# Linear attention's sums over the keys, head by head in four column tiles of the matmul array

## The chip, the cores and the metric

The kernel runs on one core of a Trainium2 chip. The metric is the device time of one execution in microseconds, the median of several runs. The core has a matmul engine (TensorE, PE in the profile, with its weight loads shown apart as PEld), three engines for elementwise work (VectorE or DVE, ScalarE or ACT, GpSimd or POOL) and a queue engine (SP) that issues most transfers. TensorE reads its operands from SBUF and writes to PSUM, which has eight banks of 128 partitions by 512 float32 values.

## The reference

Two layers with the same weights, each an attention step and a dense step. All is float32; S = 2048 rows, D = 576, H = 32 heads of Dh = 18, F = 4608.

```python
    def _A_ref(x, wqkv, w_phi, wo):
        ...
        pq = jnp.einsum("bhsd,hdf->bhsf", q, w_phi)
        pk = jnp.einsum("bhsd,hdf->bhsf", k, w_phi)
        phi_q = jnp.concatenate([_softmax(pq, axis=-1), _softmax(-pq, axis=-1)], axis=-1)
        phi_k = jnp.concatenate([_softmax(pk, axis=-1), _softmax(-pk, axis=-1)], axis=-1)
        kv = jnp.einsum("bhsf,bhsd->bhfd", phi_k, v)
        z  = jnp.einsum("bhsf->bhf", phi_k)
        num = jnp.einsum("bhqf,bhfd->bhqd", phi_q, kv)
        den = jnp.einsum("bhqf,bhf->bhq", phi_q, z)[..., None] + 1e-6
        o = num / den
        return (lambda x, *d: x.transpose(*d))(o, 0, 2, 1, 3).reshape(B, S, D) @ wo
    ...
    x = x + _A_ref(_layernorm(x, axis=-1), A_wqkv, A_w_phi, A_wo)
    x = x + _B_ref(_layernorm(x, axis=-1), B_w1, B_b1, B_w2, B_b2)
    x = x + _A_ref(_layernorm(x, axis=-1), A_wqkv, A_w_phi, A_wo)
    x = x + _B_ref(_layernorm(x, axis=-1), B_w1, B_b1, B_w2, B_b2)
```

`_B_ref` is `relu(x @ w1 + b1) ** 2 @ w2 + b2`. What the change touches is `kv` and `z`: for each head the sum over all 2048 keys of the outer products of 36 features (18 of each softmax) with 18 values and a one.

## The kernel before

The rows are worked in NB = 4 blocks of TB = 512, each of NT = 4 tiles of 128. Large products take their operands split into a high and a low part (float32r, one pass each). The products of the key sums stay in plain float32; the profile shows each of them as two loads of weights and two matmul records.

*Where the sums are made.* `make_v` multiplies a tile's rows with the weights of v and copies the result out of PSUM to a buffer `v`, in five groups of heads (four of 7 heads, 126 columns, and one of 4 heads, 72), each group with a column of ones ahead. `soft` and `soft_k` make the tile's features `e`, two softmaxes of 576 columns. `kv_tile` then multiplies, group by group, the ones and values (weights, up to 127 columns) with both softmaxes' features of that group (moved, 2 x 126 columns). This gives all pairs of heads in the group; only the blocks on the diagonal are wanted. The five products lie in three PSUM banks.

*Where they are kept.* All of layer 0's 16 tiles, and the last two blocks' 8 tiles of layer 1, add up in PSUM banks `kvp` (taken from the banks `acc0` to `acc2` that the dense layers use otherwise), which a product of zeros opens. The first two blocks of layer 1 are summed while the dense layers use these banks; each tile goes through three work tiles and is added to `kv` in SBUF by VectorE. `wtile` hands out work tiles in PSUM: two banks of the tag `w` at all times, and in turn with them those that `spare` names when the dense layers rest.

*What is made of them.* `sums_operands` stands between the last keys of a layer and its queries. It broadcasts the sums of the ones to all partitions (`sel` as weights, results `z`, copied to `zb`), turns the rest (`kt`), masks the blocks on the diagonal (`ko`) and splits them (`kbh`, `kbl`). `g_phi` divides the query features by their denominators with `zb`: VectorE and POOL each multiply, then TensorE turns the result (`g_out`).

*The order.* Generators are woven by hand (`weave`, `lagged`), and a scheduler orders the instructions of every engine by the order in which they are written where it has a choice. `barrier` writes the last keys of a layer and the first queries: names that begin with `t0` and `t1` are the barriers of the two layers. Names `m_0` to `m_3` are the dense layers of a block, `a_` a block's attention in their background, `K_` and `k_` keys, `kv_0k` to `kv_3k` the background's work tiles for the sums, `fo` the folding of w_phi into the weights at the start.

Of the kernel before, what the change touches and what calls it, by code (L numbers as in the profile page):

```python
# [21 lines left out]
def layers_kernel(  # L22
# [34 lines left out]
    HP = D // 2                      # 288  # L57
# [13 lines left out]
    # Work tiles in PSUM: two banks at all times; the banks of the dense layers too while these rest.  # L71
# [47 lines left out]
    sel = cst.tile([GW + 1, P], F32, name="sel")  # L119
    nc.vector.memset(sel, 0.0)  # L120
    nc.vector.memset(sel[0:1, :], 1.0)
    zero = cst.tile([1, P], F32R, name="zero")
    nc.vector.tensor_copy(zero, sel[32:33, :])
    zeros = zero.unsqueeze(1).to_broadcast([1, TB // P, P])
# [9 lines left out]
    def rows_twice(src, c0, n):  # L134
        """The last DT rows of src, columns c0.., on both halves of the partitions."""
# [8 lines left out]
    def g_fold(kpair):  # L144
        """Makes wf, and of it the pieces for k at once."""
# [89 lines left out]
    def g_norm(x_of, dst, name, then=None):  # L235
        """x_of(t): tile t of the rows. A step to a tile, and one for the features beyond KC * P."""
# [32 lines left out]
        def turn_rest(h):  # L269
            """The features beyond KC * P of half h of the rows."""  # L270
# [41 lines left out]
    def make_v(x, t, pair, name):  # L312
        vt = sb.tile([P, NG, GW + 1], F32, tag="v", name=f"{name}v{t}", bufs=4)
        nc.gpsimd.memset(vt[:, :, 0:1], 1.0)
        for half in range(2):
            pt = project(x, t, pair[half], f"{name}pv{half}{t}")
            a = half * HP
            while a < (half + 1) * HP:
                g, o = divmod(a, GW)
                e = min((half + 1) * HP, (g + 1) * GW)  # L320
                q = a - half * HP
                if o == 0 and a + 2 * GW <= (half + 1) * HP:
                    nc.scalar.activation(vt[:, g : g + 2, 1:],
                                         pt[:, q : q + 2 * GW].rearrange("p (g d) -> p g d", d=GW), AF.Copy)
                    a += 2 * GW
                else:
                    nc.scalar.activation(vt[:, g, 1 + o : 1 + o + e - a], pt[:, q : q + e - a], AF.Copy)
                    a = e
# [44 lines left out]
    sums = {}  # L373
    pairs = [range(g, min(g + 2, NG)) for g in range(0, NG, 2)]

    def pair_view(pt):
        return pt[: GW + 1, : 4 * GW].rearrange("p (g s f) -> p g s f", g=2, s=2)

    def kv_tile(layer, vt, e, name):
        """Adds a tile's keys: in PSUM where the dense layers rest (in the second layer for the last  # L380
        two blocks only), else in SBUF."""
        if layer not in sums:
            sums[layer] = {"kv": cst.tile([GW + 1, NG, 2, GW], F32, name=f"kv{layer}", tag="kv"), "n": 0}
# [4 lines left out]
        if n == first:  # L388
            st["ps"] = [ps_a.tile([P, TB], F32, tag=f"acc{i}", name=f"kvp{layer}{i}")
                        for i in range(len(pairs))]  # L390
            for pt, gs in zip(st["ps"], pairs):
                m = gw[gs[0]] + 1
                nc.tensor.matmul(pt[:m], zero[:, :m], zeros, start=True, stop=False)
# [423 lines left out]
```

## Time and profile before

| | |
|---|---|
| median of 3 runs | 2694.05 us (2693.41 to 2697.58) |
| span of the profiled execution | 2693.9 us |
| TensorE matmuls busy | 2614.6 us, 97% |
| TensorE weight loads busy | 2211.8 us, 82% |
| VectorE busy | 1574.4 us, 58% |
| ScalarE busy | 1065.3 us, 40% |
| GpSimd busy | 605.8 us, 22% |
| mean granted clock of TensorE | 0.989 |

The profiled execution's own time is its span of 2693.9 us; the runs' times have 2693.41 to 2697.58 beside it. The core is the only one. A row of the lines or of the time line names start, duration, engine, line, operation, what is written and read (out<-in) and the shape; a matmul's duration reaches to the modelled end of its result, so matmuls overlap and the distance between starts is what one costs. "idle before" is the idle time of the engine ahead of the group, with what ended it.

### The profile page before, as it was taken

The numbers are of one execution on the slowest core, as the hardware profiler recorded it, in microseconds if no ns is written. First come the engines' busy times: TensorE is split into PE (matmuls) and PEld (weight loads), VectorE is DVE, ScalarE is ACT, GpSimd is POOL, SyncE is SP. The second block draws the span as 40 slices with busy tenths as digits, with TensorE's granted clock in tenths as the row PEclk, the third lists the DMA queues.
The fourth block names the chain that finished last, engine by engine and source line by source line (L and its number), as shares of the span: only waits on it lengthen the run. The fifth ranks groups of instructions, "written<-read, shape, count | busy, mean of one in ns | idle before, by whom it ended". The sixth has DMA issues, their size and how long they took to land. (4 is left out here: it accounts for less than half of the span.)

```text
span 2693.9 us, 36380 instructions
## 1 busy us (share of the span) xinstructions
PE 2614.6 (97%) x13364; PEld 2211.8 (82%) x13364; DVE 1574.4 (58%) x2561; ACT 1065.3 (40%) x1837; POOL 605.8 (22%) x647
## 2 busy tenths in 40 slices
PE   6998999999999999999999989999999999999998
PEld 5997788888878888788888977888888887888887
DVE  5668944365764567547544688444854476444343
ACT  3334343344433444434443333434434343433433
POOL 1443411112311123112211333111321123111110
PEclk8998999999999999999999989999999999999999
DMA  6211233352333532334333113333432343234332
GB/s 208 89 32 45 74 110 101 98 180 84 109 112 97 171 110 82 112 97 132 113 95 109 43 57 114 87 100 102 154 118 86 102 160 97 84 101 128 98 97 74
DMA packets 289021, 280.26 MB, mean 104 GB/s; under 512 B 18697, under 2 KB 230153, under 8 KB 286793
## 3 DMA queue, kind: packets, MB, share of 16 engines
q1 hardware_dynamic: 288841, 277.92, 34.0%
q8 instruction: 105, 1.72, 0.3%
q14 instruction: 75, 0.61, 0.1%
HBM read 246.90 MB, written 30.97 MB: 103 GB/s over the span
## 5 line engine op out<-in xcount | busy, mean ns | idle before, releaser
L605 PE MATMUL m_0ph<-a_0nh,m_0h 128*128 128x512 f32 (+1 forms) x760 | 231.6, 387 | 0.0
L605 PE MATMUL m_2ph<-a_2nh,m_2h 128*128 128x512 f32 (+1 forms) x760 | 228.2, 383 | 0.1
L634 PE MATMUL m_3acc<-m_3s,m_3hb 128*128 128x512 f32 x864 | 214.2, 395 | 3.0 <-DVE m_3hb L616 1.8
L634 PE MATMUL m_0acc<-m_0s,m_0hb 128*128 128x512 f32 x864 | 214.7, 395 | 2.5 <-DVE m_0hb L616 1.1
L634 PE MATMUL m_1acc<-m_1s,m_1hb 128*128 128x512 f32 x864 | 213.3, 394 | 2.6 <-DVE m_1hb L615 1.8
L634 PE MATMUL m_2acc<-m_2s,m_2hb 128*128 128x512 f32 x864 | 213.2, 394 | 0.9 <-DVE m_2hb L615 0.7
L634 PEld LDWEIGHTS m_0acc<-m_0s,m_0hb 128*128 128x128 f32 x864 | 161.0, 188 | 43.4 <-DVE m_0hb L616 4.2
L634 PEld LDWEIGHTS m_3acc<-m_3s,m_3hb 128*128 128x128 f32 x864 | 160.9, 188 | 43.1 <-DVE m_3hb L616 4.2
L634 PEld LDWEIGHTS m_1acc<-m_1s,m_1hb 128*128 128x128 f32 x864 | 161.3, 188 | 42.1 <-DVE m_1hb L615 3.2
L634 PEld LDWEIGHTS m_2acc<-m_2s,m_2hb 128*128 128x128 f32 x864 | 161.3, 188 | 40.3 <-DVE m_2hb L615 2.2
L605 PEld LDWEIGHTS m_0ph<-a_0nh,m_0h 128*128 128x128 f32 x760 | 141.0, 190 | 28.5 <-DVE m_0h L589 0.4
L605 PEld LDWEIGHTS m_2ph<-a_2nh,m_2h 128*128 128x128 f32 x760 | 139.6, 188 | 28.8 <-DVE m_2h L589 1.0
L589 DVE TENSOR_TENSOR m_2h<-m_2r,m_2h 128x640 fp32r<-128x640 f32 x72 | 61.5, 854 | 165.4 <-ACT m_2h L588 165.4
L589 DVE TENSOR_TENSOR m_1h<-m_1r,m_1h 128x640 fp32r<-128x640 f32 x72 | 61.0, 848 | 162.5 <-ACT m_1h L588 162.5
L589 DVE TENSOR_TENSOR m_3h<-m_3r,m_3h 128x640 fp32r<-128x640 f32 x72 | 60.8, 844 | 160.8 <-ACT m_3h L588 160.8
L589 DVE TENSOR_TENSOR m_0h<-m_0r,m_0h 128x640 fp32r<-128x640 f32 x72 | 62.7, 870 | 145.9 <-ACT m_0h L588 139.2
L593 POOL TENSOR_TENSOR m_3s<-m_3r,m_3s 128x64 fp32r<-128x64 f32 x72 | 57.3, 797 | 355.2 <-ACT m_3s L591 349.6
L593 POOL TENSOR_TENSOR m_2s<-m_2r,m_2s 128x64 fp32r<-128x64 f32 x72 | 55.9, 777 | 360.9 <-ACT m_2s L591 355.4
L593 POOL TENSOR_TENSOR m_1s<-m_1r,m_1s 128x64 fp32r<-128x64 f32 x72 | 58.0, 805 | 343.8 <-ACT m_1s L591 341.7
L593 POOL TENSOR_TENSOR m_0s<-m_0r,m_0s 128x64 fp32r<-128x64 f32 x72 | 53.3, 741 | 346.3 <-ACT m_0s L591 323.8
L611 ACT ACTIVATE m_0hr<-m_0ph,b1t 128x512 f32<-128x512 f32 x72 | 49.6, 689 | 193.9 <-PE m_0ph L605 184.7
L611 ACT ACTIVATE m_3hr<-m_3ph,b1t 128x512 f32<-128x512 f32 x72 | 49.7, 690 | 192.4 <-PE m_3ph L605 187.8
(1527 smaller groups left out, 6949.8 us busy)
## 6 DMA issues: line engine op xcount, KB each, us to landing
m_3r<-in_B_w SPq DMA_DIRECT2D x72, 288.0 KB
m_2r<-in_B_w SPq DMA_DIRECT2D x72, 288.0 KB
m_0r<-in_B_w SPq DMA_DIRECT2D x72, 288.0 KB
m_1r<-in_B_w SPq DMA_DIRECT2D x72, 288.0 KB
m_3r<-in_B_w SPq DMA_DIRECT2D x72, 256.0 KB
m_2r<-in_B_w SPq DMA_DIRECT2D x72, 256.0 KB
m_0r<-in_B_w SPq DMA_DIRECT2D x72, 256.0 KB
m_1r<-in_B_w SPq DMA_DIRECT2D x72, 256.0 KB
```

The costliest lines, as they stand in the source:

```text
L589: nc.vector.tensor_sub(l1, r1, h1.bitcast(F32))
L593: nc.gpsimd.tensor_sub(s2[:, D : D + DT], r2[:, R:], s2[:, R:D].bitcast(F32))
L605: nc.tensor.matmul(ph[:, cols], a, m, start=(k == 0), stop=(k == 3 * KC + 1))
L611: nc.scalar.activation(hr, ph, AF.Relu, bias=b1t[:, f : f + 1])
L634: nc.tensor.matmul(acc[t], a[:, rows], m, start=(begin and k == 0), stop=(end and k == 2))
```

## The change

The sums are made head by head. `v` now holds for each head a one and its 18 values, 19 columns (`VW`), and 13 columns of zeros behind the last head. `kv_tile` issues 32 products in place of 5: weights are the 32 columns of `v` from a head's first on (its own 19 and 13 that belong to the next head), moved are the head's own 2 x 18 feature columns, and the result goes to 32 partitions, in the column tile q of four (`tile_position=(0, 32 * q)`). Heads 7q to 7q + 6 go to column tile q at places j = 0 to 6; heads 28 to 31 go to the four column tiles at place j = 7. All of it fills 288 columns of one bank, which a tile of keys in the background copies or adds with one instruction instead of three; in PSUM it takes one bank, and two more become work tiles (`spare`). The product of zeros is one of 288 columns instead of three of 512.

`make_v` copies each half of v with one instruction, where five were needed for both. `sums_operands` works from the new layout: `top` has a one at the first row of each column tile and broadcasts the sums of ones (12 products), 2 transposes turn both softmaxes' sums of 28 heads, and for the last 4 heads a product of VectorE (`kq`) puts each on its own quarter of partitions, and 2 products with `place` bring them to their rows.

```diff
-    sel = cst.tile([GW + 1, P], F32, name="sel")
...
+    top = cst.tile([P, NQ], F32, name="top")
...
+    place = cst.tile([P, NQ, DH], F32, name="place")
...
+    quarter = cst.tile([P, NQ], F32, name="quarter")
...
-    zeros = zero.unsqueeze(1).to_broadcast([1, TB // P, P])
+    zeros = zero[:, : 2 * DH].unsqueeze(1).to_broadcast([1, NS, 2 * DH])
...
     def make_v(x, t, pair, name):
-        vt = sb.tile([P, NG, GW + 1], F32, tag="v", name=f"{name}v{t}", bufs=4)
-        nc.gpsimd.memset(vt[:, :, 0:1], 1.0)
+        vt = sb.tile([P, H * VW + 32 - VW], F32, tag="v", name=f"{name}v{t}", bufs=4)
+        v3 = vt[:, : H * VW].rearrange("p (h d) -> p h d", d=VW)
+        nc.gpsimd.memset(v3[:, :, 0:1], 1.0)
+        nc.gpsimd.memset(vt[:, H * VW :], 0.0)
         for half in range(2):
             pt = project(x, t, pair[half], f"{name}pv{half}{t}")
...
+            nc.scalar.activation(v3[:, half * H // 2 : (half + 1) * H // 2, 1:],
+                                 pt[:, :HP].rearrange("p (h d) -> p h d", d=DH), AF.Copy)
...
+    def head(q, j):
+        return q * HG + j if j < HG else NQ * HG + q
...
+            st["ps"] = ps_a.tile([P, TB], F32, tag="acc0", name=f"kvp{layer}")
+            nc.tensor.matmul(st["ps"][:, : 2 * NS * DH], zero, zeros, start=True, stop=True)
         stay, last = n >= first, n == NB * NT - 1
-        for i, gs in enumerate(pairs):
-            pt = st["ps"][i] if stay else wtile(f"{name}k{i}")
-            po = pair_view(pt)
-            for g in gs:
-                nc.tensor.matmul(po[: gw[g] + 1, g - gs[0], :, : gw[g]], vt[:, g, : gw[g] + 1],
-                                 e[:, :, g * GW : g * GW + gw[g]],
-                                 start=not stay, stop=(not stay or (last and g == gs[-1])))
...
+        pt = st["ps"] if stay else wtile(f"{name}k")
+        po = pt[:, : 2 * NS * DH].rearrange("p (s j f) -> p s j f", s=2, f=DH)
+        for j in range(NS):
+            for q in range(NQ):
+                h = head(q, j)
+                nc.tensor.matmul(po[32 * q : 32 * q + 32, :, j], vt[:, h * VW : h * VW + 32],
+                                 e[:, :, h * DH : (h + 1) * DH], start=not stay, stop=True,
+                                 tile_position=(0, 32 * q), skip_group_check=True)
+        if stay and not last:
+            return
+        if (last and first == 0) or n == 0:
+            nc.scalar.activation(kv, po, AF.Copy)
+        else:
+            nc.vector.tensor_add(kv, po, kv)
...
+        for s in range(2):
+            pt = wtile(f"z{layer}{s}")
+            for q in range(NQ):
+                nc.tensor.matmul(pt[:, q * GW : (q + 1) * GW], top[:, q : q + 1].to_broadcast([P, P]),
+                                 kv[:, s, :HG], start=True, stop=True)
...
+            nc.tensor.transpose(pt[:GW, :P], kv[:, s, :HG].rearrange("p j f -> p (j f)"), ident)
...
-    spare["tags"] = ["acc3", "acc4", "h"]
+    spare["tags"] = ["acc1", "acc2", "acc3", "acc4", "h"]
```

On TensorE, at the first tile of keys of the first layer, before and after (`n_1p` is a transpose of the next block's norm, `v_0pv` the product for the tile's v):

```order
L265 MATMUL n_1p_653<-ident,n_1n_565 128x128 x4
L399 MATMUL kvp_672<-K_0_0e,v_0v_473 127x252 x2
L399 MATMUL kvp_673<-K_0_0e,v_0v_473 127x252 x2
L399 MATMUL kvp_674<-K_0_0e,v_0v_473 73x2x72
L308 MATMUL v_0pv_685<-w0v0h,n_0h 128x288
```

```order
L284 MATMUL n_1p_662<-ident,n_1n_576 128x128 x4
L408 MATMUL kvp_681<-K_0_0e,v_0v_486 32x2x18 x32
L327 MATMUL v_0pv_718<-w0v0h,n_0h 128x288
L327 MATMUL v_0pv_718<-w0v0l,n_0h 128x288
L327 MATMUL v_0pv_718<-w0v0h,n_0l 128x288
```

The place is the same; five products to three banks have become 32 to one.

On TensorE, in the second layer, in the background of a block's dense layers (`m_0acc` and `m_0ph` are their products), before and after:

```order
L627 MATMUL m_0acc_8068<-m_0hb_8738,m_0s_7_8716 128x512 x2
L399 MATMUL kv_2_0k_8857<-k_2K0e,v_2v_8372 127x252 x2
L399 MATMUL kv_2_0k_8861<-k_2K0e,v_2v_8372 127x252 x2
L605 MATMUL m_0ph_8880<-a_0nh,m_0h_9_8873 128x512
L605 MATMUL m_0ph_8880<-a_0nl,m_0h_9_8873 128x512
L399 MATMUL kv_2_0k_8865<-k_2K0e,v_2v_8372 73x2x72
L605 MATMUL m_0ph_8880<-a_0nh,m_0h_9_8873 128x512 x2
```

```order
L649 MATMUL m_0acc_8558<-m_0hb_9220,m_0s_7_9198 128x512 x2
L408 MATMUL kv_2_0k<-k_2K0e,v_2v_8862 32x2x18 x32
L627 MATMUL m_0ph_9385<-a_0nh,m_0h_9_9378 128x512
L627 MATMUL m_0ph_9385<-a_0nl,m_0h_9_9378 128x512
L627 MATMUL m_0ph_9385<-a_0nh,m_0h_9_9378 128x512 x2
```

The tile's third part, which stood two products of the dense layers later, is gone; the tile is one run.

On TensorE, from the last keys of the first layer on (`t0q2qp` are products for the queries of another block), before and after:

```order
L399 MATMUL kvp_674<-k_3K3e,t0v_2245 73x2x72
L425 MATMUL z_2333<-kv_671,sel 128x252 x2
L440 MATMUL kt_2346<-ident,kv_671 126x127
L425 MATMUL z_2338<-kv_671,sel 128x252 x2
L425 MATMUL z_2342<-kv_671,sel 128x2x72
L440 MATMUL kt_2346<-ident,kv_671 126x127 x3
L440 MATMUL kt_2355<-ident,kv_671 126x127 x4
L440 MATMUL kt_2364<-ident,kv_671 72x73 x2
L308 MATMUL t0q2qp_2401<-t0q1h,n_2h 128x288
```

```order
L408 MATMUL kvp_681<-k_3K3e,t0v_2575 32x2x18 x32
L327 MATMUL t0q2qp_2883<-t0q0h,n_2h 128x288
L327 MATMUL t0q2qp_2883<-t0q0l,n_2h 128x288
L327 MATMUL t0q2qp_2883<-t0q0h,n_2l 128x288
L327 MATMUL t0q2qp_2883<-t0q0h,n_2h 128x288
L327 MATMUL t0q2qp_2883<-t0q0l,n_2h 128x288
L428 MATMUL z_2740<-kv_680,top 128x126 x4
L428 MATMUL z_2746<-kv_680,top 128x126 x4
L437 MATMUL z_2752<-kv_680,top 128x2x18 x4
L449 MATMUL kt_2758<-ident,kv_680 126x128
L449 MATMUL kt_2764<-ident,kv_680 126x128
```

Five products for the other block's queries now stand ahead of the broadcasts, which are twelve and no longer stand among the transposes; of these two are left.

More of the change, by code (lines that the diff above doesn't have):

```diff
@@ L57, in layers_kernel @@
     HP = D // 2
+    VW = DH + 1
+    NQ = P // 32
+    NS = H // NQ
+    assert VW <= 32 and NS == HG + 1 and NG == NQ + 1
     cst = ctx.enter_context(tc.tile_pool(name="cst", bufs=1))
@@ L373, in layers_kernel @@
     sums = {}
-    pairs = [range(g, min(g + 2, NG)) for g in range(0, NG, 2)]
-    def pair_view(pt):
-        return pt[: GW + 1, : 4 * GW].rearrange("p (g s f) -> p g s f", g=2, s=2)
+    def head(q, j):
+        return q * HG + j if j < HG else NQ * HG + q
     def kv_tile(layer, vt, e, name):
         if layer not in sums:
-            sums[layer] = {"kv": cst.tile([GW + 1, NG, 2, GW], F32, name=f"kv{layer}", tag="kv"), "n": 0}
+            sums[layer] = {"kv": cst.tile([P, 2, NS, DH], F32, name=f"kv{layer}", tag="kv"), "n": 0}
         st = sums[layer]
@@ L388, in kv_tile @@
         if n == first:
[L389 to L393, printed above, removed]
-        stay, last = n >= first, n == NB * NT - 1
-        for i, gs in enumerate(pairs):
-            pt = st["ps"][i] if stay else wtile(f"{name}k{i}")
-            po = pair_view(pt)
-            for g in gs:
-                nc.tensor.matmul(po[: gw[g] + 1, g - gs[0], :, : gw[g]], vt[:, g, : gw[g] + 1],
-                                 e[:, :, g * GW : g * GW + gw[g]],
-                                 start=not stay, stop=(not stay or (last and g == gs[-1])))
-            w = gw[gs[0]]
-            src = po[: w + 1, : len(gs), :, :w]
-            dst = kv[: w + 1, gs[0] : gs[-1] + 1, :, :w]
-            if stay and not last:
-                continue
-            if (last and first == 0) or n == 0:
-                if i % 2:
-                    nc.vector.tensor_copy(dst, src)
-                else:
-                    nc.scalar.activation(dst, src, AF.Copy)
-            else:
-                nc.vector.tensor_add(dst, src, dst)
+            st["ps"] = ps_a.tile([P, TB], F32, tag="acc0", name=f"kvp{layer}")
+            nc.tensor.matmul(st["ps"][:, : 2 * NS * DH], zero, zeros, start=True, stop=True)
+        stay, last = n >= first, n == NB * NT - 1
+        pt = st["ps"] if stay else wtile(f"{name}k")
[12 more added lines that the diff above has]
+            nc.vector.tensor_add(kv, po, kv)
     def sums_operands(layer):
@@ L433, in sums_operands @@
-        last = NG - 1
-        for i, batch in enumerate([[(0, g) for g in range(last)], [(1, g) for g in range(last)],
-                                   [(0, last), (1, last)]]):
-            w, n = gw[batch[0][1]], len(batch)
-            pt = wtile(f"kt{layer}{i}")
-            p3 = pt[:, : n * (w + 1)].rearrange("p (j m) -> p j m", m=w + 1)
-            for j, (s, g) in enumerate(batch):
-                nc.tensor.transpose(p3[:w, j], kv[: w + 1, g, s, :w], ident[: w + 1, : w + 1])
-            own = sb.tile([P, TB], F32, tag="hr", name=f"ko{layer}{i}", bufs=2)
-            own = own[:w, : n * w].rearrange("p (j m) -> p j m", m=w)
-            nc.vector.tensor_mul(own, p3[:w, :, 1:], mask[:w, :w].unsqueeze(1).to_broadcast([w, n, w]))
-            hi, lo = (k[:w, i, :last, :w] if i < 2 else k[:w, :, last, :w] for k in (kbh, kbl))
+        last = NG - 1
@@ L445, in sums_operands, with keep @@
+        p3 = pt[:, : 2 * NQ * DH].rearrange("p (s q f) -> p s q f", s=2, q=NQ)
+        for q in range(NQ):
+            nc.tensor.matmul(p3[:, :, q], top[:, q : q + 1].to_broadcast([P, P]), kv[:, :, HG],
+                             start=True, stop=True)
+        nc.scalar.activation(zb[:, :, NQ * GW :], p3.rearrange("p s q f -> p s (q f)"), AF.Copy)
+        def keep(own, parts):
+            hi, lo = parts
             nc.scalar.activation(hi, own, AF.Copy)
             nc.vector.tensor_sub(lo, own, hi.bitcast(F32))
+        for s in range(2):
+            pt = wtile(f"kt{layer}{s}")
+            nc.tensor.transpose(pt[:GW, :P], kv[:, s, :HG].rearrange("p j f -> p (j f)"), ident)
+            own = sb.tile([P, TB], F32, tag="hr", name=f"ko{layer}{s}", bufs=2)
+            own = own[:GW, : NQ * GW].rearrange("p (q j d) -> p q j d", q=NQ, j=HG)
+            src = pt[:GW, :P].rearrange("p (q d) -> p q d", q=NQ)[:, :, 1 : 1 + DH]
+            nc.vector.tensor_mul(own, src.unsqueeze(2).to_broadcast([GW, NQ, HG, DH]),
+                                 mask.rearrange("p (j d) -> p j d", j=HG).unsqueeze(1)
+                                 .to_broadcast([GW, NQ, HG, DH]))
+            keep(own.rearrange("p q j d -> p q (j d)"), [k[:, s, :last] for k in (kbh, kbl)])
@@ new lines, in sums_operands @@
+        w = gw[last]
+        own = sb.tile([P, TB], F32, tag="hr", name=f"kq{layer}", bufs=2)
+        own = own[:, : 2 * w].rearrange("p (s q f) -> p s q f", s=2, q=NQ)
+        nc.vector.tensor_mul(own, kv[:, :, HG].unsqueeze(2).to_broadcast([P, 2, NQ, DH]),
+                             quarter.unsqueeze(1).unsqueeze(3).to_broadcast([P, 2, NQ, DH]))
+        pt = wtile(f"kt{layer}2")
+        p3 = pt[:w, : 2 * w].rearrange("p (s n) -> p s n", s=2)
+        for s in range(2):
+            nc.tensor.matmul(p3[:, s], own[:, s].rearrange("p q f -> p (q f)"),
+                             place.rearrange("p q d -> p (q d)"), start=True, stop=True)
@@ L447, in sums_operands @@
+        keep(p3, [k[:w, :, last, :w] for k in (kbh, kbl)])
         sums[layer].update(zb=zb, kb=(kbh, kbl))
```

47 lines of the change are left out of this document (19 added, 28 removed).

## The prediction

> **What bounds the kernel now.** I read the page's busy shares first, then the clock and the slices, then windows along the span, then the lines of the key sums by tile, and last the waits of the two stretches between keys and queries.
>
> ```profile
> PE 2614.6 (97%) x13364; PEld 2211.8 (82%) x13364; DVE 1574.4 (58%) x2561; ACT 1065.3 (40%) x1837; POOL 605.8 (22%) x647
> PE   6998999999999999999999989999999999999998
> PEclk8998999999999999999999989999999999999999
> ```
>
> TensorE (PE) is busy for 97% of the span and its clock is at full grant nearly throughout. Only three places show less than nine tenths: the start, 200 to 300 us, and 1550 to 1650 us. So the time is TensorE's work plus 79 us in which it stands idle. What the change takes from TensorE, or from what TensorE waits for, comes off the end.
>
> The key sums, by windows on their line alone (window, length, PE busy and records, weight loads, clock, DMA):
>
> ```profile
> 0.00:218.00 218.00, 25.51 (x120) 20.68 (x120) 0.95 0.32 104
> 218.00:232.00 14.00, 8.11 (x40) 6.88 (x40) 1.00 0.21 58
> 640.00:700.00 60.00, 9.15 (x40) 6.78 (x40) 1.00 0.43 130
> 960.00:1022.00 62.00, 9.61 (x40) 6.89 (x40) 0.94 0.39 121
> 1470.00:1500.00 30.00, 8.54 (x40) 6.89 (x40) 1.00 0.45 139
> 1538.00:1552.00 14.00, 8.11 (x40) 6.88 (x40) 1.00 0.18 53
> ```
>
> That is 320 records, ten to a tile of 128 keys, so 32 tiles. Five float32 products make ten records, so each product is two loads of weights and two matmul records. The busy time there overlaps its neighbours; what a tile takes from TensorE is the distance between the starts around it:
>
> ```profile
> 79.48 2.11 PE L399 MATMUL kvp<-K_1e,v_0v 128*127 128x252 f32 x10
> 81.43 0.60 PE L265 MATMUL n_1p<-ident,n_1n 128*128 128x128 f32 x4
> ```
>
> One tile costs 81.43 - 79.48 = 1.95 us. It moves 4 x 252 + 144 = 1152 columns twice, so 2304 columns in 1.95 us, 0.85 ns for each column of a record.
>
> **The change, part by part.** *Key sums.* In place of 10 records with 73 to 127 columns of weights come 32 products, so 64 records, each with 32 columns of weights and 36 moved columns. That is 32 x 36 = 1152 columns again, twice: moved one after the other they cost the same 1.95 us, and the change gains only if the four column tiles work side by side, and loses if something other than the moving sets the step. No row shows a matmul in a column tile or one this narrow. The nearest rows are these:
>
> ```profile
> 16.41 1.86 PEld L178 LDWEIGHTS fo<-phi,ft 126*128 126x128 f32 x16 [1.03 <-DVE ft L169]
> 18.19 0.47 PEld L167 LDWEIGHTS fp<-ident,fr 128*126 128x126 f32 x4
> 18.63 0.53 PEld L178 LDWEIGHTS fo<-phi,ft 72*128 72x128 f32 x4
> 18.73 0.56 PE L178 MATMUL fo<-phi,ft 72*128 72x72 f32 x4
> 813.76 0.11 PEld L521 LDWEIGHTS a_0pt<-ident,a_0Q0e 128*72 128x72 f32 x1 [0.29 <-DVE a_0fl L523]
> 813.79 0.12 PEld L521 LDWEIGHTS a_0pt<-ident,a_0Q1e 128*72 128x72 f32 x1
> 268.86 0.27 PE L521 MATMUL t0opt<-ident,t0fQ3e 128*126 128x128 f32 x1
> 268.89 0.48 PE L535 MATMUL t0opn<-t0ofh,kbh 126*126 126x512 f32 x1
> ```
>
> In the folding of w_phi 16 loads of 128 columns take 18.19 - 16.41 = 1.78 us, 0.111 each. Where only 72 columns are moved (18.73) the four records still fill 0.56 us beside loads that fill 0.53: the load sets the step there and the moving is hidden. Loads do get shorter with fewer columns: those of 72 columns at 813.76 start 0.03 apart. So a load of 32 columns is about 0.111 x 32 / 128 = 0.028 us, and moving 36 columns is 36 x 0.85 = 0.030 us. The shortest step from one matmul to the next with other weights is 0.03 (268.86 to 268.89).
>
> Bounds for a tile: all four column tiles side by side, 64 x 0.030 / 4 = 0.49 us; load and moving never together, 64 x 0.058 = 3.7 us. I exclude a step of 0.111 (7.1 us), because the loads of 72 columns show that the load shrinks. Between them I take 64 x 0.027 = 1.73 us: both parts overlap as they do in the folding, and the step is the last pair of rows, which lies at or a little under load and moving alone. That is 0.22 us less for each tile. It counts where TensorE has no slack: in all tiles except the last three of each layer, behind which TensorE waits for others in any case (below). 26 x 0.22 = -6 us, between -38 (26 x 1.46) and +46 (26 x 1.75).
>
> *Waits for PSUM in the background of the dense layers.* There the tile needs three of the two work banks, now one:
>
> ```profile
>   DVE kv L413: 4.7, 3
> 969.73 1.86 PE L399 MATMUL kv_0k<-k_2K0e,v_2v 128*127 128x252 f32 x8
> 975.08 0.76 PE L399 MATMUL kv_0k<-k_2K0e,v_2v 128*73 128x144 f32 x2 [3.02 <-DVE kv L413]
> 965.00:985.00 20.00, 16.98 (x67) 13.75 (x66) 10.47 (x14) 6.00 (x9) 4.78 (x4) 0.83 0.18 53
> 985.00:1005.00 20.00, 20.00 (x111) 17.47 (x110) 15.32 (x18) 9.42 (x14) 5.78 (x6) 1.00 0.39 128
> ```
>
> TensorE stood 4.7 us in three places for the adds of the first two parts, 3.0 of them at 975.08, queued on VectorE. Around that wait the clock fell to 0.83 over 20 us, a half grant for 6.8 us; at most 3.8 of these lie outside the idle time and cost 1.9. Together 6.6. One add is left to each tile, which can still hold a bank when VectorE is late, so I take -6 (0 to -6.6). VectorE's adds shrink from 1152 columns to 288 on the way, which hides behind TensorE.
>
> *Zero fill.* Three products of 512 columns become one of 288:
>
> ```profile
> 1477.42 0.96 PE L393 MATMUL kvp<-zero 1*127 1x512 f32 x3
> 1478.31 2.21 PE L399 MATMUL kvp<-k_0K0e,v_prevv 128*127 128x252 f32 x10
> ```
>
> 0.89 us becomes some 0.15: -0.7. The first layer's lies at 2.4 us, ahead of the first rows, and costs nothing either way. The new constants (memsets and selections on VectorE and POOL) lie there too, under the wait for the first rows of x.
>
> *From the last keys to phi(q), twice.* The chain is copy of the sums, broadcast products, copies to zb, then POOL's first product:
>
> ```profile
> 227.87 2.11 PE L399 MATMUL kvp<-k_3K3e,t0v 128*127 128x252 f32 x10
> 229.74 1.16 ACT L359 ACTIVATE t0fQ3e<-t0fQ3e 128x1152 f32<-128x1152 f32 x1 [2.60 <-DVE t0fQ3e L357]
> 230.81 0.75 ACT L411 ACTIVATE kv<-kvp 127x504 f32<-127x504 f32 x2
> 232.32 0.68 DVE L409 COPY kv<-kvp 127x504 f32<-127x504 f32 x1
> 235.65 1.41 POOL L493 TENSOR_TENSOR t0fm<-t0fQ0e,zb 128x576 f32<-128x576 f32 x1 [5.50 <-ACT zb L432]
> 1548.22 2.11 PE L399 MATMUL kvp<-k_lastK3e,t1v 128*127 128x252 f32 x10
> 1551.27 1.35 DVE L361 TENSOR_REDUCE t1fQ3r<-t1fQ3e 128x64 f32<-128x1152 f32 x1 [0.92 <-ACT t1fQ3e L359]
> 1552.66 1.48 DVE L413 TENSOR_TENSOR kv<-kvp,kv 127x504 f32<-127x504 f32 x3
> 1557.06 1.41 POOL L493 TENSOR_TENSOR t1fm<-t1fQ0e,zb 128x576 f32<-128x576 f32 x1 [9.33 <-ACT zb L432]
> L336 ACT ACTIVATE k_3ks<-k_3kp 128x288 f32<-128x288 f32 x16 | 6.5, 405 | 11.6 <-PE k_3kp L308 11.6
> L413 DVE TENSOR_TENSOR kv<-kv_3k,kv x6: 303/672/676, 688.2 to 1018.8; 127x504 f32<-127x504 f32 x4, 73x144 f32<-73x144 f32 x2
> ```
>
> In the first layer TensorE is through with the last keys at 229.98, but ACT's exponential ends at 230.90 and VectorE's sum over it at 232.28. This is the cover of the last three tiles: a faster tile moves nothing there, a slower one costs only what exceeds 0.9 us (in the second layer, 1550.33 to 1552.62, 2.3). After the change one copy of 288 columns (0.41 by the copy of a half of k) stands right behind the exponential and waits for nothing of VectorE; it is done at 231.3. The 12 broadcast products load 128 columns each, 24 records at the folding's 0.111 are 2.7 us, to 234.0; the last copy to zb then takes 0.3, and POOL starts at about 234.5 in place of 235.65. In the second layer one add of 288 columns (0.45, between 0.30 for 144 and 0.67 for 504) follows the sum at 1552.66, the products end at 1555.8, and POOL starts at 1556.2 in place of 1557.06. Behind it VectorE and POOL set the pace, so the start passes on: -2 in all (0 to -3). Fewer transposes (2 for 10) free TensorE earlier, under a wait for phi(q) that stays. The 2 new products that place the last heads need a VectorE product of 144 columns first; they stand behind some thirty matmuls of the next queries and are hidden.
>
> *Copies of v.* Five short copies on ACT become two of 288 columns; two more banks are free while the keys are made.
>
> ```profile
>   ACT t0v L327: 1.9, 1
>   ACT t1v L327: 1.6, 1
> ```
>
> That is all TensorE waits for these copies, 3.5 us; I take half, -1.5 (0 to -3.5). POOL's second memset for v stands in the queue with the first, which waits for the products that last read this buffer in both versions; nothing on TensorE waits for it before the copies do.
>
> **The sum.** -6 - 6 - 0.7 - 2 - 1.5 = -16 us against the profiled span of 2693.9: 2678. The median of the runs shown is 2694.05, 0.15 above that span, so I leave it at 2678. A measurement of this kernel can tell 0.2%, 5.4 us, from no change.
>
> **The rivals.** *Side by side.* The four column tiles overlap and a tile takes 0.49 to 1.2 us (two at a time, 1.0, lies within). For it speaks that one tile's loading and moving use a quarter of the array; against it that load and matmul alternate on one queue, and that two records of one product share a column tile and must follow each other. The sums then give -20 to -38 and the total is 2646 to 2664. The Trainium skill, "TensorE: Matmul & The Clock Gate" (Part 3), has three column tiles at 512 moved columns run 2.38 times as fast as one by one. By that factor a tile would take 0.82 us and the total be 2655, an estimate; no run so far shows a column tile.
>
> *A drain at each change of tile shape.* What it would do, from rows: the step between key records is 0.21 us, but one takes 0.375 to its end:
>
> ```profile
> L399 PE MATMUL kvp<-K_1e,v_0v x10: 285/375/377, 79.5 to 81.3; 128*127 128x252 f32 x8, 128*73 128x144 f32 x2
> ```
>
> If TensorE had to run empty when it enters and leaves the column tiles, 0.165 us of tail and a bare load of 0.111 would show, 0.28 twice for a tile: 26 x 0.55 = +14. With one column tile at a time and a step of 0.033 (0.030 and a tenth, as no step meets its bound), the sums give +4 and the total is 2684 + 4 + 14 = 2702 (2690 to 2706). The Trainium skill, "TensorEngine Tiling (Array Packing)" (Key Properties), says that a change of the tiling mode drains the engine, which speaks against this change.
>
> *Load and moving one after the other.* Then the step is 0.058 us, a tile takes 3.7, and 26 tiles give +46; the last three tiles of both layers exceed their cover by 4.3 and 2.9 us more. 2684 + 46 + 7 = 2737. It ends on the other side: with the other terms at -10, a tile of 2.33 us decides, a step of 0.036. Against it speak the rows of the folding, where a load runs beside the matmul ahead; for it, that those have the whole array, with a second set of weights behind the first. The same page of the Trainium skill, "TensorE: Matmul & The Clock Gate" (Part 3), says that loads run beside matmuls in flight only in other groups of rows; the four column tiles share theirs.
>
> *The idle time only moves.* The waits of 6.6, 2 and 1.5 us come back elsewhere, since VectorE is as late as before, and only the sums gain: 2688, no change.
>
> **How the numbers follow.** My forecast (a step near 0.027 and the waits gone, 2670 to 2688) has 0.30, side by side 0.25, the drain with one tile at a time 0.20, load and moving in line 0.15, idle time that only moves 0.10. Faster than 2688.7: 0.30 + 0.25 and half of the last, 0.60. Slower than 2699.4: the 0.15 and 0.12 of the drain's 0.20, 0.27; the rest, 0.13, is no change. The range of 2642 to 2720 takes in the first two, the drain and the last, and leaves out the case in line and little else.
>
> **What would show it.** In the profile after: the distance from a key tile's first matmul to the next work (1.95 before): 1.7 as I say, 0.5 to 1.2 side by side, 2.6 with drains, 3.7 in line. A gap at its first record or at the first behind it is the drain. The waits for VectorE's adds ahead of key records should be under 1 us in all, the clock near 975 us at full grant, POOL's first product some 1 us earlier behind the last keys. The prediction is wrong if the step lies beyond 0.036 us, or if the tiles run side by side.

## The result, and the profile after

| | before | after |
|---|---|---|
| median of the runs | 2694.2 us (2693.4 to 2697.6) | 2654.6 us (2653.0 to 2654.9) |
| span of the profiled execution | 2693.9 us | 2653.1 us |
| TensorE busy | 2614.6 us | 2574.8 us |
| idle time of TensorE | 72.1 us | 71.4 us |

The ratio is 0.985 (95% interval 0.9836 to 0.9864): 39.7 us less, where 16 were forecast. The time lies inside the range, in the part of the rival that lets the column tiles run side by side. The idle row adds up the idle time ahead of every matmul (span less busy time, which the prediction puts at 79 us, is 78.3 after). It stayed, since waits that went came back in other places (below); on balance the gain is busy time. Busy shares and slices of the page after:

```profile
PE 2574.8 (97%) x15108; PEld 2179.3 (82%) x15108; DVE 1560.5 (59%) x2545; ACT 1056.4 (40%) x1735; POOL 614.9 (23%) x683
PE   6998899999999999999999989999999999999998
PEclk8998999999999999999999989999999999999999
```

1744 more records on TensorE take 39.8 us less. The tile that the prediction showed at 79.48, on the time line of TensorE after:

```profile
74.11 0.60 PE L284 MATMUL n_1p<-ident,n_1n 128*128 128x128 f32 x4
74.55 0.38 PE L294 MATMUL n_1p<-ident,n_1e 128*128 128x128 f32 x2
74.86 0.77 PE L408 MATMUL kvp<-K_1e,v_0v 128*32 128x36 f32 x64
75.56 0.66 PE L284 MATMUL n_1p<-ident,n_1n 128*128 128x128 f32 x4
```

The row ahead of the tile before the change, which the prediction does not show:

```profile
79.27 0.38 PE L275 MATMUL n_1p<-ident,n_1e 128*128 128x128 f32 x2
```

From the first record to the next work it is 75.56 - 74.86 = 0.70 us, 1.95 before. In the raw starts 64 records span 0.575 us, 0.0091 from one to the next, a third of my 0.027. Two pairs of rows show the change of shape. The two transposes ahead take 0.31 us to the first key record (74.55 to 74.86), before 0.21 (79.27 to 79.48): 0.1 more at the entry. By the raw starts the same 0.09 to 0.10 stands behind the products of the keys and of v (0.22 against 0.13) and of the dense layers (0.33 against 0.23). And from the last key record to the next work it is 0.128 us by the raw starts, where the records of the tile stood 0.009 apart: 0.12 at the exit.

The windows on the key sums' line after, beside those shown of before:

```profile
0.00:218.00 218.00, 12.44 (x1024) 10.54 (x1024) 0.96 0.33 105
640.00:700.00 60.00, 2.32 (x192) 1.98 (x192) 1.00 0.42 130
960.00:1022.00 62.00, 2.32 (x192) 1.97 (x192) 1.00 0.40 125
```

Three tiles in each of the two windows of the dense layers fill 2.32 us, 0.77 a tile with the modelled end. The clock is at full grant there; around the wait that stood at 975 us before, too:

```profile
965.00:985.00 20.00, 20.00 (x221) 16.95 (x214) 16.93 (x19) 10.92 (x15) 7.36 (x6) 1.00 0.46 167
985.00:1005.00 20.00, 20.00 (x172) 17.51 (x171) 10.87 (x16) 6.81 (x12) 5.86 (x9) 1.00 0.53 146
```

TensorE is busy for all of both windows. No wait for VectorE's adds is left ahead of a background tile. But among the waits of TensorE after stand new ones, ahead of the key sums:

```profile
PE kvp L408 <- POOL K_0e L380: 4.3, 3, 1.6
PE kvp L408 <- ACT t1v L338: 3.0, 2, 2.4
PE kvp L408 <- ACT t0v L338: 1.9, 1, 1.9
PE kvp L408 <- POOL K_2e L380: 1.2, 2, 0.6
```

5.5 us for POOL's features `K_` in the first keys (1.5 before), and 4.9 for ACT's copies of v, which wait ahead of key records now and ahead of the next queries before (3.5).

### The profile page after: what moved, and what is told of

Read it like the earlier page. It is cut to its first block, busy times and chain, and to the rows that moved or that the text cites. A ratio compares the mean times of both kernels' runs of the same rounds, so it can differ in the third digit from the quotient of the medians.

```text
span 2653.1 us, 39728 instructions
## 1 busy us (share of the span) xinstructions
PE 2574.8 (97%) x15108; PEld 2179.3 (82%) x15108; DVE 1560.5 (59%) x2545; ACT 1056.4 (40%) x1735; POOL 614.9 (23%) x683
## 5 line engine op out<-in xcount | busy, mean ns | idle before, releaser
L656 PEld LDWEIGHTS m_0acc<-m_0s,m_0hb 128*128 128x128 f32 x864 | 160.6, 188 | 43.5 <-DVE m_0hb L638 4.4
L656 PEld LDWEIGHTS m_1acc<-m_1s,m_1hb 128*128 128x128 f32 x864 | 161.3, 188 | 41.3 <-DVE m_1hb L638 3.1
```

Source lines behind the costliest of these rows:

```text
L656: nc.tensor.matmul(acc[t], a[:, rows], m, start=(begin and k == 0), stop=(end and k == 2))
```

## The experiments

Three rounds against the kernel before for each, if nothing else is said; differences "to after" are between medians of different rounds. The kernel before had medians of 2693.7 to 2695.9 us in these rounds and 2694.2 beside after, so such a difference is good to about 2 us.

**The eight products of a column tile one after another.**

```diff
-        for j in range(NS):
-            for q in range(NQ):
+        for q in range(NQ):
+            for j in range(NS):
```

> The 32 products of a tile of keys in another order: all eight of a column tile one after the other, then the next column tile's; the same work and sums. If the gain comes from column tiles that work side by side, neighbours now share a tile and each record waits for the one before: 64 records at about 0.030 us, a tile of 1.9 to 2.1 us in place of 0.58, and 26 to 32 tiles give back 36 to 45 us: 2690 to 2700. If narrow records are simply cheap (0.009 us each, whatever tile they go to), the tile stays at 0.58 us and the time at 2655.

Measured: 2675.2 us (2673.1 to 2678.0), ratio 0.9926 (0.9911 to 0.994), 20.6 more than after. The same place on the time line:

```profile
74.54 0.38 PE L294 MATMUL n_1p<-ident,n_1e 128*128 128x128 f32 x2
74.85 1.98 PE L408 MATMUL kvp<-K_1e,v_0v 128*32 128x36 f32 x64
76.76 0.66 PE L284 MATMUL n_1p<-ident,n_1n 128*128 128x128 f32 x4
```

Instructions and shapes are the same, only the order differs: 1.91 us for a tile instead of 0.70, 1.78 from first to last record. That is 0.028 for each record, nearly my 0.027. So the price of a record in one column tile was right, and what I had put second, that the column tiles overlap, is what happens: 1.78 / 0.575 = 3.1 times as fast. The rival that has load and moving in line (0.058) falls as well. And this kernel, whose tile costs what it did before (1.91 against 1.95, and 0.1 more at the entry), is still 19 to 21 us faster than the kernel before: that half of the gain has other sources.

**Two column tiles in turn, then the other two.**

```diff
-        for j in range(NS):
-            for q in range(NQ):
+        for j, q in [(j, q) for half in (0, 2) for j in range(NS) for q in (half, half + 1)]:
```

> The order of the products again: column tiles 0 and 1 in turn for the first half, then 2 and 3 in turn. Side by side, two at a time: 64 x 0.030 / 2, a tile of about 1.0 us, 0.4 more than with four, 10 to 13 us for all: 2665 to 2668. If narrow records are cheap in any order: 0.58 us and 2655.

Measured: 2661.0 us (2659.7 to 2663.1), ratio 0.9873 (0.9858 to 0.9888), 6.5 more than after.

```profile
74.20 1.15 PE L408 MATMUL kvp<-K_1e,v_0v 128*32 128x36 f32 x64
75.28 0.66 PE L284 MATMUL n_1p<-ident,n_1n 128*128 128x128 f32 x4
```

1.08 us to the next work, 0.95 from first to last: 0.015 for each record. One column tile, two, four: 0.028, 0.015, 0.009. The overlap is of column tiles, nearly whole with two and a little less with four. The page "TensorE: Matmul & The Clock Gate" (Part 3) of the Trainium skill has three at 512 columns run 2.38 times as fast; these rows lie in line with it at 36 columns, 1.9 times with two and 3.1 with four.

**Half the moved columns.** Only the features of the first softmax are summed, and ones stand for the second's sums.

```diff
-                nc.tensor.matmul(po[32 * q : 32 * q + 32, :, j], vt[:, h * VW : h * VW + 32],
-                                 e[:, :, h * DH : (h + 1) * DH], start=not stay, stop=True,
+                nc.tensor.matmul(po[32 * q : 32 * q + 32, 0, j], vt[:, h * VW : h * VW + 32],
+                                 e[:, 0, h * DH : (h + 1) * DH], start=not stay, stop=True,
```

> The key sums with 18 moved columns, not 36: the second softmax is left out of them, so half of each head's sums stay zero or one. If moving the columns sets the step of four column tiles side by side, a tile's 64 records shrink from 0.575 us to 0.30 to 0.35. If the loads of 32 columns set it (0.028 each, four at a time, 64 x 0.007 = 0.45), 0.45 to 0.55. If the queue's step of 0.009 sets it, 0.57.

Measured, a single run: 2646.8 us.

```profile
L409 PE MATMUL kvp<-K_0e,v_0v x64: 183/185/206, 65.0 to 65.6; 128*32 128x18 f32 x64
```

First to last record it is 0.556 us in the raw starts, against 0.575 with 36 columns. Moving is not what sets the step with four column tiles; the load of 32 columns or a fixed step of the queue is, and no run here parts these two. The time fell by 7.7 us all the same, which 32 x 0.02 can't explain. By the traces 0.8 and 3.3 us of it lie in the two stretches from the barrier's first product for v to the next dense layers, where VectorE and ACT have less to do, and 2.3 in the dense layers behind the first of them. Why they gain so much stays open.

**One more change of tile shape in each tile, and its control.** Both add a full-array product of one row of zeros by 36 columns, one between the halves of a tile, one behind it.

```diff
+            if j == NS // 2:
+                nc.tensor.matmul(pt[:, 2 * NS * DH : 2 * NS * DH + 2 * DH], zero, zeros[:, 0],
+                                 start=True, stop=True, skip_group_check=True)
```

> After, with one full-array product of 36 columns between the two halves of every key tile: one row of zeros times the zero row, into 36 columns of the same bank that nothing reads, so the result is as before. Each tile then leaves the column tiles and enters them once more. If every change of tile shape makes TensorE run empty (0.09 us more ahead of the first record, 0.12 and a bare load of 0.11 behind the last), a tile takes 0.32 us more and the product itself: some 0.35 x 32 = 11 us on TensorE, 26 of them where it has no slack, 2662 to 2666; the two halves of the tile (0.28 us each) then stand 0.35 us apart. If the change of shape costs nothing, only the product's own step shows, 0.03 x 32 = 1 us, and the time is that of the same product behind the tile: about 2656.

> After, with the same product of zeros behind each tile's last record, where TensorE leaves the column tiles in any case. It adds two records and no change of tile shape: 0.03 to 0.1 us a tile, 1 to 3 us in all, 2655 to 2658. If it costs as much as the product in the middle, the price there is the product's and not that of changing shape.

In one point the expectation was wrong: started between the tiles, that product makes the next records of the whole bank write instead of add, so in the first layer's keys and the second's last ones these two kernels' sums are not those of all keys. The instructions are as described. The Trainium skill, "PSUM — Partial Sum Buffer" (The four PSUM rules), has it so: a product that opens a sum resets the marks of its whole bank, whichever columns it writes.

Measured: in the middle 2660.8 us (2659.9 to 2661.6), ratio 0.9874 (0.9859 to 0.9888); behind 2658.4 (2657.7 to 2659.4), ratio 0.9865 (0.985 to 0.988). In the middle:

```profile
74.35 0.38 PE L294 MATMUL n_1p<-ident,n_1e 128*128 128x128 f32 x2
74.66 0.47 PE L411 MATMUL kvp<-K_1e,v_0v 128*32 128x36 f32 x32
75.06 0.28 PE L407 MATMUL kvp<-zero 1*128 1x36 f32 x1
75.27 0.47 PE L411 MATMUL kvp<-K_1e,v_0v 128*32 128x36 f32 x32
75.67 0.66 PE L284 MATMUL n_1p<-ident,n_1n 128*128 128x128 f32 x4
```

And behind, in the background of the dense layers:

```profile
647.43 0.77 PE L408 MATMUL kv_1k<-k_3K1e,v_3v 128*32 128x36 f32 x64
648.13 0.28 PE L411 MATMUL kv_1k<-zero 1*128 1x36 f32 x1
648.34 0.50 PE L629 MATMUL m_2ph<-a_2nh,m_2h 128*128 128x512 f32 x1
```

In the middle a tile takes 1.01 us instead of 0.70, 0.31 more, where 0.35 was expected. Behind it, the product adds 0.21 (648.34 - 648.13), so it was no cheap control: in the trace it is one record, not two, but its load has 128 columns of weights, and such loads stood 0.111 apart in the folding. In the middle it is 0.21 as well from the product to the tile's second half (75.06 to 75.27). At this entry nothing shows beyond what the product costs ahead of full-array work; whether the entry is free there or hidden under the product, these two runs don't tell. What is left of the 0.31, 0.10, is the one exit more: 0.13 by the raw starts from the last record of the first half to the product, where records stand 0.009 apart. The two times differ by 2.4 us, and 32 x 0.10 are 3.2. With the 0.1 at the entry behind other work, read above, this fits a drain at each change of shape, which the Trainium skill, "TensorEngine Tiling (Array Packing)" (Key Properties), states without a price. My rival's 0.55 for a tile was too dear, and 11 us for the run in the middle (6.3 measured) too, since not all that TensorE loses reaches the end: 6.3 of 32 x 0.31 = 9.9. With two column tiles it is 6.5 of 12.0, with one 20.6 of 38.5.

**The sums two tiles late in the first layer's keys (five rounds).** In after a tile's sums stand one tile behind its features; here two.

```diff
-            if pending:
-                kv_tile(0, *pending.pop())
+            if len(pending) > 1:
+                kv_tile(0, *pending.pop(0))
```

> The changed kernel, but in the first layer a tile's key sums are issued two tiles after its features were begun, not one. In the changed kernel TensorE waits 5.5 us in all for POOL's last product of the features ahead of key records (4.3 for K_0e, 1.2 for K_2e; 1.5 before the change). If these waits eat part of the gain, they go and the time is 2649 to 2651. If VectorE, ScalarE and POOL set the pace of the key tiles anyway, or the next stretch takes the time back, 2654 to 2656.

Measured: 2646.9 us (2645.5 to 2648.2), ratio 0.9825 (0.981 to 0.9839): 7.7 less than after, and the fastest of the kernels that sum everything. The waits for `K_0e` and `K_2e` are gone; ahead of key records TensorE waits only for ACT's v and 0.6 us for nothing shown:

```profile
PE kvp L408 <- ACT t1v L338: 2.9, 2, 2.4
PE kvp L408 <- ACT t0v L338: 1.5, 1, 1.5
```

**The same lag with one column tile at a time, and with the kernel before.**

> The key tiles two tiles late, as in the run at 2646.9, and the eight products of each column tile one after another, as in the serial run (2675.2). If the shorter tile lost part of its 1.2 us to TensorE waiting for POOL's and VectorE's features, and the lag takes that wait away, side by side is worth more here than the 20.6 us between serial and after: 24 to 26 tiles x 1.2 = 28 to 31, so 2675 to 2678, with the lag worth nothing to the serial order. If something else in those stretches limits it, or the lag helps both orders alike, the difference stays 20.6 and the time is 2667.

> The kernel before, with the first layer's key tiles two tiles late instead of one. Its TensorE waits only 1.5 us for POOL's features there, so if the lag pays only by removing those waits, 2692 to 2694, no difference. If the lag brings something else (a better order of the other engines around the tile), it is worth some 8 us here too: 2686.

Measured: in the serial order 2671.0 us (2669.3 to 2671.4), ratio 0.9909 (0.9893 to 0.9926), 4.2 less than without the lag. In the kernel before 2690.0 (2687.5 to 2691.8), ratio 0.9981 (0.9972 to 0.9991) to 2694.9: 4.9 less. So the lag is worth 4 to 5 us to any version, which neither of my readings had. In the traces 3.4 us (before) and 3.8 (serial) are gained between the first products for v of blocks 0 and 1; 2.0 and 1.8 of them are left at the barrier, and the rest of the gain comes behind it. Why stays open. What the lag is worth beyond that with short tiles is some 3 us: side by side against one by one is 24.1 us with the lag and 20.6 without. From the first product for v to the first of the barrier, over 12 tiles, the traces have 137.2 us serial and 122.7 side by side with the lag, 14.5 less or 1.2 a tile, all of it; without the lag 139.0 and 128.8, 10.2 less.

**The spare banks as before.**

```diff
-    spare["tags"] = ["acc1", "acc2", "acc3", "acc4", "h"]
+    spare["tags"] = ["acc3", "acc4", "h"]
```

> The changed kernel with the work tiles of the kernel before (acc3, acc4 and h to spare; the two banks that came free stay unused). If the two more banks bring the 4.6 us by which the folding at the start is now done earlier, the first product for v starts near 52 us again and the time is 2658 to 2661. If they bring nothing, 2655 within 2.

Measured: 2659.2 us (2657.3 to 2660.9), ratio 0.9864 (0.9848 to 0.9881), 4.6 more than after (3.0 when each is set against the kernel before of its own rounds). The first products for v stand among the folding's in after, and behind it here. After, then with fewer banks:

```profile
47.51 0.38 PE L327 MATMUL v_0pv<-w0v0h,n_0h 128*128 128x288 f32 x1
47.72 1.46 PE L197 MATMUL fo<-phi,ft 126*128 126x126 f32 x12
```

```profile
52.92 0.61 PE L197 MATMUL fo<-phi,ft 126*128 126x126 f32 x4
53.28 0.38 PE L327 MATMUL v_0pv<-w0v0h,n_0h 128*128 128x288 f32 x1
```

The gain arises there: at the first product for the second block's v, the kernel with fewer banks is still 4.7 us behind. It doesn't last whole: 1.8 us are left at the second layer's first product for v (1444.9 against 1443.1). Some 3 more are lost in the dense layers behind the second barrier, whose first block takes 273.0 us, as in the kernel before (272.9), instead of 270.1, with 2.4 us more idle time of TensorE. The edit takes the banks away in both layers, and no run parts the two. I had costed the two banks at nothing.

**v copied in five pieces again.**

```diff
-            nc.scalar.activation(v3[:, half * H // 2 : (half + 1) * H // 2, 1:],
-                                 pt[:, :HP].rearrange("p (h d) -> p h d", d=DH), AF.Copy)
+            for a, b in (((0, 14), (14, 16)), ((16, 21), (21, 28), (28, 32)))[half]:
+                nc.scalar.activation(v3[:, a:b, 1:],
...
```

> The changed kernel with v copied out of PSUM in five pieces a tile, as before (14, 2, 5, 7 and 4 heads), not two. The prediction gave the two copies 1.5 us (0 to 3.5): 2656 to 2658. If ScalarE has slack wherever they stand, no change, 2655 within 1.5.

Measured: 2656.3 us (2653.0 to 2657.9), ratio 0.9853 (0.9839 to 0.9868). 1.8 more than after, which the runs don't part from none. In these rounds the kernel before was slower too: set against it, this kernel gains 39.6 us and after 39.7, and their profiled spans differ by 0.4. So my -1.5 is not borne out.

**Three work tiles and three adds for each background tile.**

```diff
+        for a, b in ((0, NS),) if stay else ((0, 3), (3, 6), (6, NS)):
+            pt = st["ps"] if stay else wtile(f"{name}k{a}")
...
+                nc.vector.tensor_add(kv[:, :, a:b], po, kv[:, :, a:b])
```

> The changed kernel, but in the background of the dense layers a tile of keys goes through three work tiles in PSUM and three adds again (places j 0 to 2, 3 to 5, 6 and 7). If the waits for these banks were worth what the prediction says, 6.6 us of idle time and half clock come back: 2660 to 2662. If the shorter tile has made them harmless, 2655 to 2657.

Measured: 2665.7 us (2662.3 to 2666.9), ratio 0.9896 (0.9879 to 0.9912), 11 more than after.

```profile
955.91 0.64 PE L408 MATMUL kv_0k<-k_2K0e,v_2v 128*32 128x36 f32 x48
956.48 0.50 PE L627 MATMUL m_0ph<-a_0nh,m_0h 128*128 128x512 f32 x1
956.82 0.40 PE L627 MATMUL m_0ph<-a_0nl,m_0h 128*128 128x512 f32 x1
958.21 0.34 PE L408 MATMUL kv_0k<-k_2K0e,v_2v 128*32 128x36 f32 x16 [1.00 <-DVE kv L416]
958.48 0.73 PE L627 MATMUL m_0ph<-a_0nh,m_0h 128*128 128x512 f32 x2
```

The last part waits for VectorE's add (2.4 us over the three such waits, 4.7 before), and because it stands behind two products of the dense layers, the tile enters and leaves the column tiles twice (eight times the 0.1 at the entry and 0.12 at the exit are an estimated 1.8 us). The trace, of the fastest of the four runs, has 7.3 of the 11 us (2660.4 against 2653.1). The eight background tiles' stretch is 4.9 us longer than after (895.8 against 890.9, from the dense layers' second block to the second layer's first product for v). The other 2.4 are lost from the second barrier on, and there the dense layers' first block takes 273.0 us instead of 270.1, with 2.4 us more idle time, as with fewer banks. So the waits for the work tiles account for 2.4 us only; of the 4 us that the slower runs have beyond the trace nothing is known.

**All of this undone at once**: serial order, fewer banks, five copies and three work tiles. What remains of the change is the sums head by head in a tile of 1.9 us, the new `sums_operands`, the shorter fill with zeros, and adds and copies of 288 columns in all instead of 1152.

> Four parts undone at once: column tiles one after the other, two banks fewer, v copied in five pieces, three work tiles and adds in the background. If their prices add up (20.6 and 4.6 and 1.8 as measured, 6.6 as forecast), 2687 to 2690, and 4 to 7 us are left for the stretch from the last keys to the queries and the fill with zeros. If they overlap, so that one wait stands where another was taken away, 2677 to 2683 and the rest is worth 11 or more.

Measured: 2683.7 us (2682.6 to 2685.0), ratio 0.9961 (0.9947 to 0.9976), 10 less than before. Undone singly these four cost 20.6 + 4.6 + 1.8 + 11 = 38, together 29: with tiles of 1.9 us the three parts cost nothing in the background (its stretch is 898.9 us, 899.7 in serial). Among its waits:

```profile
PE kv_0k L410 <- DVE kv L418: 0.6, 1, 0.6
PE kv_2k L410 <- DVE kv L418: 0.5, 2, 0.3
```

4.7 us have become 1.1 with three parts still there. So with a tile as long as before the shorter adds took most of that wait away, and the one bank was not needed for it; with the short tile the three parts still waited 2.4 us (above). By the traces the background stretch is 7.3 us shorter than before, the stretch around the first layer's last keys 3.1 (from the first product for its v to the next dense layer), that of the second 3.6.

## Why the prediction was right or wrong

| term | forecast | measured | from |
|---|---|---|---|
| key sums, side by side | -6 | -20.6 | serial against after |
| waits in the background | -6 | -7.3 | all undone against before |
| last keys to phi(q) | -2 | -6.7 | the same, 3.1 + 3.6 |
| zero fill | -0.7 | -0.3 | the same, by the stretch of the trace |
| copies of v | -1.5 | 0 to -1.8 | five pieces |
| spare banks | 0 | -4.6 | banks as before |

Together -39.5 to -41.3, beside -39.7 measured. That this closes is in part luck. The rows mix medians of different rounds with stretches of single traces, and the three from undone add up to 14.3, where its median is 10 below the kernel before: its start and first keys are 2.3 us longer by the trace, which no row has, and its trace gains 2 us more than its median.

**Key sums.** The step that failed is the choice of 64 x 0.027 for a tile: it has the records of the four column tiles follow each other. They run side by side, 0.009 us apart, so the tile took 0.70 us instead of 1.73. I had given this case a chance of 0.25 and held against it that load and matmul alternate on one queue and that both records of a product share a column tile. The runs with one, two and four show that neither prevents it.

The price of a record in one column tile did come out, 0.028, but the rows that I took it from don't bear it. These stand right behind the matmul at 268.89 and the load at 813.79:

```profile
269.21 0.27 PE L521 MATMUL t0opt<-ident,t0fQ2e 128*72 128x128 f32 x1
813.90 0.12 PEld L521 LDWEIGHTS a_0pt<-ident,a_0Q2e 128*72 128x72 f32 x1
```

The matmul takes 0.32 to the next, so the 0.03 ahead of it is no step that could be repeated. The next load of 72 columns stands 0.11 behind, as far as those of 128, beside matmuls that move 128 columns. That a load shrinks with its columns, and that a step of 0.111 was out, these rows did not show. As far as it rests on them, 0.028 came out by luck; what did stand behind it was the moving, 36 x 0.85 = 0.031.

The estimate of 2655 in this rival met the time by luck as well: it has 29 us for the sums, where 20.6 were measured, and 10 for everything else, where some 19 were.

**Which tiles count.** That the tiles behind which TensorE waits in any case gain nothing was right: from the first product for v in the barriers to the next dense layers, after is 2.3 and 0.9 us longer than serial. (In the first, among others, TensorE waits 1.9 us for ACT's v and 2.1 more for VectorE ahead of `t0q3qp`, and the broadcasts run at half the clock, below.) I named three in each layer; four stand in these stretches. The other 24 are worth 24 x 1.2 = 29. Of these 4.2 went to new waits for POOL's features in the first keys (5.5 in after, 1.4 in serial), 3.2 to the two stretches, about 1 each to the background and to the start, and some 1.4 came back between the barrier and the background: 20.6. What is late next I had not asked for the first keys, and that is what the lag of two tiles answers.

**Drain.** A price at each change of shape is real, 0.1 at the entry and some 0.12 at the exit; my 0.55 for a tile was two and a half times that. The rival's time of 2702 fell with its serial step. Break-even at a step of 0.036 was never near.

**Background.** The size was right, a part of the reason not: I had put it down to the one bank, and with a tile of 1.9 us the shorter adds do most of it (1.1 us of wait left with three parts); with the short tile one bank is worth 2.4 us of wait more. The clock near 975 us is at full grant, as forecast.

**From the last keys to phi(q).** POOL's first product stands 0.9 us earlier after the barrier's first product for v in the first layer (45.94 us behind it, 46.88 before) and 2.8 in the second (43.5, 46.35). About 1 was forecast; the first came by other steps than mine. The exponential, the broadcast products, POOL's product, and the windows (TensorE only) over the products:

```profile
215.72 1.17 ACT L370 ACTIVATE t0fQ3e<-t0fQ3e 128x1152 f32<-128x1152 f32 x1 [0.79 <-DVE t0fQ3e L368]
216.80 0.39 ACT L414 ACTIVATE kv<-kvp 128x288 f32<-128x288 f32 x1
217.24 3.67 PE L428 MATMUL z<-kv,top 128*128 128x126 f32 x16 [0.74 <-ACT kv L414]
220.75 0.98 PE L437 MATMUL z<-kv,top 128*128 128x36 f32 x8
221.57 0.41 PE L449 MATMUL kt<-ident,kv 128*126 128x128 f32 x2
222.19 1.43 POOL L515 TENSOR_TENSOR t0fm<-t0fQ0e,zb 128x576 f32<-128x576 f32 x1 [6.26 <-ACT zb L439]
```

```profile
216.00:217.00 1.00, 0.50 (x4) 1.00 0.08 18
218.00:219.00 1.00, 1.00 (x7) 0.50 0.88 308
219.00:220.00 1.00, 1.00 (x7) 0.50 0.76 254
221.00:222.00 1.00, 1.00 (x11) 1.00 0.93 323
```

The copy stands right behind the exponential, as forecast. But 24 records take 4.3 us (217.24 to 221.57) instead of 2.7, because the clock is granted by half: 16 of them stand 0.22 apart, where the folding had 0.111. In the serial run, with a clock of 1.00 from 224 to 228 us, the same 24 records take 2.7 us (224.41 to 227.12), so the price was right for the full clock. The kernel before had its half grant there too (0.64 from 233 to 235). From the exponential's end to POOL it is now 5.3 us, 4.75 before. The gain came from an exponential that ended earlier within the stretch (40.6 us behind its first product for v, 42.1 before). On the whole the two stretches are 1.4 and 4.8 us shorter in after than before, four short tiles in each included. I had taken a price at full clock into a stretch that I knew begins with waits.

**Zero fill and copies of v** were small. The fill came out at half its price; for the copies no gain is shown. The waits for ACT's copies did not go away, they moved ahead of the key records (4.9 us, 3.5 before).

**The banks** are a term that I left out. I noted that two more come free while the keys are made and gave that no price, though the first of the page's 40 slices shows TensorE at six tenths: I did not ask who else stands there waiting for a work tile.

## What to carry to other kernels

Where many small products share their rows and each fills 32 columns or fewer, write them so that neighbours in the order go to different column tiles: the same instructions ran 3.1 times as fast in turn as one column tile after another. Enter the column tiles in long runs, since entering and leaving them costs about 0.2 us together, and look at once for what feeds the shorter step, here the features, which needed one tile more of lead for another 7.7 us (4 to 5 of them also with the long tile). When a layout is changed, price also what it frees (banks, columns that another engine adds) for whoever stands in line for it.

## What the runs showed of the hardware that was not expected

- Records of different column tiles start 0.009 us apart with four in turn, 0.015 with two, 0.028 with one; halving the moved columns from 36 to 18 changes the 0.0091 to 0.0088.
- A product of one row and 36 moved columns, with a load of 128 columns of weights, costs 0.21 us between other products, as much as moving 250 columns at 0.85 ns.
- After waits of 1.9 and 0.74 us within 4.5 us, with no wait longer than that, the clock was granted by half from 217 to about 220.6 us. The Trainium skill, "TensorE: Matmul & The Clock Gate" (Part 1), has the grant follow free-running windows of 3.4 us; the length of the slow stretch agrees, and the rows show that it takes no single wait of that length. Nor does the sum of the waits decide: with the lag of two tiles, waits of 1.46, 0.59 and 0.62 us within 4.5 us at the same place left the clock at 1.00 (from 209 to 213 us). Windows that run free would explain both; no run here shows it.
- A product that opens a sum in unused columns of a bank made the sums beside it start anew; the results of the two runs with such products came out with a relative error of 0.996.
